# Each output tile stored as two transfers of 64 rows instead of one of 2 x 64 rows

## The chip, the cores and the metric

The kernel runs on one core of a Trainium2 chip. The metric is the time of one execution on the device in microseconds; the time of before is the median of three runs. One further execution was recorded by the hardware profiler, and all rows below are from it. TensorE (PE, with PEld for its weight loads), VectorE (DVE), ScalarE (ACT) and GpSimd (POOL) compute; SyncE (SP) issues nearly all DMAs, which 16 DMA engines carry out. "SPq" and "ACTq" in a row are the queues of SP and ACT, with their DMA issues; "q1" is the DMA queue that SP's issues go to, "q10" that of ACT's.

## The reference, cut to what matters

A gated linear recurrence over 768 steps for 4 batches and 8 heads of 40 elements, and then a feed-forward block with a rational activation on the 3072 tokens:

```python
for t in range(S):                       # for every batch and head
    m_new = np.maximum(f_gate[:, :, t] + m, i_gate[:, :, t])
    C = f_stab * C + i_stab * outer(v[t], k[t])
    n = f_stab * n + i_stab * k[t]
    y[:, :, t] = sigmoid(o_gate[t]) * (C @ q[t]) / np.maximum(np.abs(n @ q[t]), 1.0)
x = y.transpose(0, 2, 1, 3).reshape(B * S, H * D)      # [3072, 320]
h = x @ w_in                                           # [3072, 2048]
g = (a[0] + a[1]*h + a[2]*h**2 + a[3]*h**3) / (1 + abs(b[0])*abs(h) + abs(b[1])*h**2 + 1e-6)
out = g @ w_out                                        # [3072, 320], rows (batch, position)
```

## The kernel before, in words

The recurrence is computed in chunks of 64 positions, as matrix products with decay factors. The feed-forward block runs over twelve groups of 256 tokens (`SIZES`), each in eight steps over 256 of the 2048 hidden columns: a product into `ph` with `w_in`, some ten operations on ACT, DVE and POOL for the activation, and a product that adds into `po` with `w_out`. Weights and activations are kept as a high and a low part, so that each product is several matmuls. Loads, recurrence and feed-forward of different groups are interleaved by the text `ORDER`, a list of steps written out beforehand; every engine works through its own steps in that order, and SP too: a DMA that waits holds up the DMAs behind it. SP's DMAs use eight semaphores in turn, so that an issue also waits until the transfer eight places ahead has landed.

A group covers two batches and 128 positions. It ends with two output tiles `ot` (t = 0 and 1), each of 128 partitions and 320 columns: partitions 0 to 63 hold 64 positions of one batch, partitions 64 to 127 the same positions of the next. In `out` the rows of the two batches lie 768 rows apart. Step `ev` (`f_ev`) moves `po` from PSUM to the tile, on ACT for most groups; step `ed` (`f_ed`) issues its store from SP. For the very last tile of the last group `ev` is on DVE, and `f_ev` calls `f_ed` itself with ACT's queue. Line 34 of the profile is the helper that records every operation in order; the store from ACT has line 1353, in `f_ed`. At the end the program waits on SP for all stores (line 1469). A flag read from the input chooses between two versions of the program; the rows are of the version that ran.

Of the kernel before, what the change touches and what calls it, by code (L numbers as in the profile page):

```python
# [374 lines left out]
def _program(  # L375
# [16 lines left out]
    nc = _Ordered(tc)  # L392
    B, H, S, D = q.shape
    DM, DFF = w_in.shape
    P = 128
    L = 64
# [48 lines left out]
    def ring(pool, tag, shape, name, dt=F32, at=None):  # L445
        k = plan.slot[tag] if at is None else at
        return pool.tile(shape, dt, tag=f"{tag}{k}", name=name, bufs=1)
# [767 lines left out]
    def feed_forward(n, i):  # L1215
        d = {}
# [83 lines left out]
        def parts_of(t):  # L1300
            return [(t, 0, 0, DM)] if t < 8 - BANKS else [(0, DM, 0, 512 - DM), (1, DM, 512 - DM, DM)]
# [28 lines left out]
        def f_ev(t, engine):  # L1330
            ot = d["ot", t] = ring(fp, "ot", [P, DM], f"ot{n}_{t}")
            for b, at, lo, hi in parts_of(t):
                to, po = ot[:, lo:hi], PO[n, half][b][:, at : at + hi - lo]
                if split:
                    nc.vector.scalar_tensor_tensor(
                        to, po, pa[:, 3:4] if square else 1.0, PT[n][:, t, lo:hi], op0=ALU.mult, op1=ALU.add
                    )
                elif engine == "DVE":
                    nc.vector.tensor_scalar(to, po, pa[:, 3:4] if square else 1.0, None, op0=ALU.mult)
                elif square:  # L1340
                    nc.scalar.activation(to, po, AF.Copy, scale=pa[:, 3:4])
                else:
                    nc.scalar.copy(to, po)
            if engine == "DVE" and not split:
                f_ed(t, nc.scalar)

        def f_ed(t, queue):
            m = firsts_of[n] + t // 2
            blk, b = divmod(2 * m, B)
            rows = out.rearrange("(b s) e -> b s e", b=B)[  # L1350
                b : b + 2, blk * P + t % 2 * L : blk * P + (t % 2 + 1) * L
            ]
            queue.dma_start(rows, d["ot", t])

        k = f"{n}_{i}"
        a0, a1 = (ps[:, 2:3], ps[:, 1:2]) if square else (pa[:, 0:1], pa[:, 1:2])
# [1 line left out]
        def add(name, engine, cost, fn, r=(), w=(), new=(), part=None, **kw):  # L1358

            def own(x):  # L1360
                if x not in ("h", "ha", "w", "p", "gH", "gL"):
                    return x
                if part is None or not last:
                    return f"{x}{k}"
                return f"h{k}p{part}" if x == "h" else f"{x}{k}.{part}"

            plan.add(
                f"{name}{'half' if last and part is not None else ''}_{k}", engine, cost, fn,
                [own(x) for x in r], [*(own(x) for x in w), f"turn {name}"],
                [(own(x).split(".")[0], t) for x, t in new], **kw,  # L1370
            )
# [10 lines left out]
        for j in range(2):  # L1382
            f = chunk(j)
            add("f1", "PE", 0.9, lambda j=j: f_f1(j), w=["h"], new=[("h", ("h", BANKS))] if j == 0 or last else (), part=j,
                r=[*xs, f"wi{f // 2}", f"wi{f // 2}.l",
                   *(f"wj{f % 8 // 4}{x}" for x in ("", ".x", ".l"))])
# [24 lines left out]
        if i == NS - 1:  # L1411
            for t in range(groups):
                o = f"ot{n}_{t}"
                e = "DVE" if split or t == groups - 1 and n == len(SIZES) - 1 else "ACT"
                add("ev", e, 0.32, lambda t=t, e=e: f_ev(t, e), r=[f"pt{n}.{t}"] if split else [],
                    w=[*(po[b] for b, *_ in parts_of(t)), o], new=[(o, ("ot", BUFS["ot"]))], lag=2.5)
                if e == "ACT" or split:
                    add("ed", "SP", 0.6, lambda t=t: f_ed(t, nc.sync), r=[o], lag=2.5)

    stg = ctx.enter_context(tc.tile_pool(name="stage", bufs=2))  # L1420
    ap1 = ctx.enter_context(tc.tile_pool(name="att1", bufs=1))
# [17 lines left out]
    for n, i in steps + [(n, i) for n in range(SPLIT, len(SIZES)) for i in range(NS)]:  # L1439
        feed_forward(n, i)  # L1440
# [33 lines left out]
```

## Time and profile before

| what | value |
|---|---|
| runs | 507.96, 509.19, 509.38 us; median 509.19 us |
| profiled execution, span from first to last instruction | 504.4 us |
| TensorE busy | 478.4 us, 95% of the span |
| output stores | 24 of 160 KB: 23 issued from SP, 1 from ACT |
| first and last of SP's stores issued at | 126.4 us and 493.1 us |

The profiled execution is given by its span alone; its own time, with what lies before the first and after the last instruction, is not recorded. The runs lie 3.5 to 4.9 us above the span. A DMA issue has a start and a length on the queue of its engine; the transfer itself is seen only in the views of the DMA engines, which show their busy share and the bytes moved.

### The profile page before, as it was taken

What the parts mean: (1) busy time and instruction counts of PE and PEld (TensorE: products, weight loads), DVE (VectorE), ACT (ScalarE), POOL (GpSimd) and SP (SyncE); (2) the same over time, 40 slices, a digit from 0 to 9 for tenths busy, and PEclk for the clock granted to TensorE, in tenths of its full rate; (3) what the DMA queues carried; (4) which work ended last, traced back from release to release, by engine and by line L of the source; (5) the groups of instructions that cost most, each with busy time, mean ns of one, the idle gap of its engine ahead of it and who ended that gap; (6) DMA issues with size and microseconds to landing.
All of it is one profiled execution on the core that took longest, in us unless ns stands there. A gap on an engine that the chain in (4) does not pass through costs nothing.

```text
span 504.4 us, 14192 instructions
## 1 busy us (share of the span) xinstructions
PE 478.4 (95%) x5631; PEld 462.5 (92%) x5631; DVE 420.4 (83%) x716; ACT 402.1 (80%) x698; POOL 385.4 (76%) x365
## 2 busy tenths in 40 slices
PE   5988889999999999999999999999999999999990
PEld 5977778999999999999999999999999999999980
DVE  7787999999998898897868887796977998687890
ACT  3488999898986886879887799797788778779960
POOL 2767689998868878877888788878868887967760
PEclk9989999999999999999999999999999999999996
DMA  6899998503543335333326522320332030000001
GB/s 177 192 198 232 234 219 163 101 12 66 106 111 77 71 80 105 82 73 83 52 72 116 115 58 59 79 57 6 64 97 44 3 74 3 18 10 2 27 1 33
DMA packets 119438, 42.54 MB, mean 84 GB/s; under 512 B 103618, under 2 KB 111874, under 8 KB 119362
## 3 DMA queue, kind: packets, MB, share of 16 engines
q1 hardware_dynamic: 119232, 41.37, 38.0%
q8 instruction: 46, 0.75, 0.6%
q14 instruction: 30, 0.25, 0.1%
q10 hardware_dynamic: 130, 0.16, 0.1%
HBM read 36.90 MB, written 4.10 MB: 81 GB/s over the span
## 4 chain that ended last, share of the span: by engine, by line
PE 72%; DVE 8%; ACT 5%; DMA 4%; POOL 3%; issue 3%; SPq 3%; DVEq 0%; ACTq 0%; POOLq 0%
PE ph L34 30%; PE po L34 29%; PE y L34 4%; PE kq L34 3%; SPq L34 3%; PE ow L34 3%; PE ps L34 2%; DMA kr<-in_k_dram 2%; POOL p L34 1%; PE px L34 1%; DMA rawj<-in_moe_w_in_dram 1%; ACT ph L34 1%; DVE w L34 1%; DVE gH L34 1%; DMA rawi<-in_moe_w_in_dram 1%
## 5 line engine op out<-in xcount | busy, mean ns | idle before, releaser
L34 POOL TENSOR_TENSOR p<-p,w 128x512 f32<-128x512 f32 (+1 forms) x97 | 127.6, 1316 | 59.7 <-DVE w L34 55.8
L34 PE MATMUL ph<-xk,wi 128*128 128x256 f32 x1152 | 167.8, 281 | 0.5 <-DVE zo L34 0.5
L34 PEld LDWEIGHTS ph<-xk,wi 128*128 128x128 f32 x1152 | 149.8, 188 | 1.9 <-PE ph L34 0.7
L34 POOL TENSOR_TENSOR w<-w,ha 128x512 f32<-128x512 f32 (+1 forms) x97 | 127.1, 1316 | 10.0 <-ACT w L34 9.9
L34 PE MATMUL po<-wo,gH 128*128 128x320 f32 x768 | 134.6, 312 | 0.0
L34 PEld LDWEIGHTS po<-wo,gH 128*128 128x128 f32 x768 | 115.1, 188 | 0.8
L34 DVE SCALAR_TENSOR_TENSOR gL<-p,ps,ph 128x512 fp32r<-128x512 f32 (+1 forms) x97 | 71.3, 735 | 22.0 <-POOL p L34 19.8
L34 DVE SCALAR_TENSOR_TENSOR w<-w,gH 128x512 f32<-128x512 f32 (+1 forms) x97 | 81.7, 842 | 4.1
L34 ACT ACTIVATE ph<-w,cd 128x512 f32<-128x512 f32 (+1 forms) x97 | 66.6, 687 | 22.7 <-POOL w L34 12.4
L34 DVE SCALAR_TENSOR_TENSOR gH<-p,ps,ph 128x512 fp32r<-128x512 f32 (+1 forms) x97 | 71.3, 735 | 13.9 <-ACT ph L34 12.9
L34 ACT ACTIVATE w<-ha,ba 128x512 f32<-128x512 f32 (+1 forms) x97 | 78.6, 813 | 2.3
L34 ACT ACTIVATE ha<-ph 128x512 f32<-128x512 f32 (+1 forms) x97 | 57.5, 593 | 27.4 <-PE ph L34 26.6
L34 PE MATMUL po<-wo,gL 128*128 128x320 f32 x384 | 77.2, 314 | 0.8 <-DVE gL L34 0.8
L34 DVE SCALAR_TENSOR_TENSOR p<-p,ps,ph 128x512 f32<-128x512 f32 (+1 forms) x97 | 70.5, 734 | 7.2 <-ACT p L34 6.9
L34 ACT ACTIVATE p<-ph,ps 128x512 f32<-128x512 f32 (+1 forms) x97 | 65.2, 679 | 0.3
L34 PEld LDWEIGHTS po<-wo,gL 128*128 128x128 f32 x384 | 59.2, 188 | 2.3 <-DVE gL L34 1.7
L34 ACT ACTIVATE ph<-ph 128x512 f32<-128x512 f32 (+1 forms) x97 | 56.0, 578 | 2.2
L34 PE MATMUL ph<-xk,wY 128*128 128x256 f32 x192 | 53.5, 279 | 0.0
L34 PE MATMUL ph<-xk,wj 128*128 128x256 f32 x192 | 53.4, 278 | 0.0
L34 PEld LDWEIGHTS ph<-xk,wj 128*128 128x128 f32 x192 | 36.1, 188 | 0.0
L34 PEld LDWEIGHTS ph<-xk,wY 128*128 128x128 f32 x192 | 36.1, 188 | 0.0
L34 PE MATMUL hot<-ident 128*128 128x128 f32 x180 | 25.0, 297 | 4.0 <-DVE flag_out L370 4.0
(136 smaller groups left out, 650.2 us busy)
## 6 DMA issues: line engine op xcount, KB each, us to landing
rawo<-in_moe_w_out_dram SPq DMA_DIRECT2D x8, 640.0 KB
ab<-scrA SPq DMA_DIRECT2D x40, 128.0 KB
rawi<-in_moe_w_in_dram SPq DMA_DIRECT2D x8, 512.0 KB
kr<-in_k_dram SPq DMA_DIRECT2D x24, 160.0 KB
vb<-in_v_dram SPq DMA_DIRECT2D x48, 80.0 KB
og<-in_o_gate_dram SPq DMA_DIRECT2D x48, 80.0 KB
qn<-in_q_dram SPq DMA_DIRECT2D x24, 160.0 KB
out_dram<-ot SPq DMA_DIRECT2D x23, 160.0 KB
```

Source lines behind the costliest of these rows:

```text
L34: made = fn(*args, **kwargs)
```

## The change

`f_ed` takes a list of queues, one for each batch, and issues one store of 64 rows for each: rows 0 to 63 of the tile to one batch, rows 64 to 127 to the next. From SP both go out one behind the other; for the last tile the first half goes out from ACT and the second from SP.

```diff
             if engine == "DVE" and not split:
-                f_ed(t, nc.scalar)
-
-        def f_ed(t, queue):
+                f_ed(t, (nc.scalar, nc.sync))
+
+        def f_ed(t, queues):
             m = firsts_of[n] + t // 2
             blk, b = divmod(2 * m, B)
-            rows = out.rearrange("(b s) e -> b s e", b=B)[
-                b : b + 2, blk * P + t % 2 * L : blk * P + (t % 2 + 1) * L
-            ]
-            queue.dma_start(rows, d["ot", t])
+            at = blk * P + t % 2 * L
+            for j, queue in enumerate(queues):
+                rows = out.rearrange("(b s) e -> b s e", b=B)[b + j, at : at + L]
+                queue.dma_start(rows, d["ot", t][j * L : (j + 1) * L])
...
-                    add("ed", "SP", 0.6, lambda t=t: f_ed(t, nc.sync), r=[o], lag=2.5)
+                    add("ed", "SP", 0.6, lambda t=t: f_ed(t, (nc.sync, nc.sync)), r=[o], lag=2.5)
```

SP's issues at the end of the program, from the loads of the last chunks of the recurrence (`kr`, `qn`, `vb`, `ab`) to the last DMA of this version; `ot_0` and `ot_1` are the two output tiles of a group, and the numbers behind them only tell tiles apart. Before:

```order
L34 DMA out_dram<-ot_1_5859 2x64x320
L34 DMA vb_62<-in_v_dram 64x8x40 x2
L34 DMA ab_6447<-scrA 64x2x256 x2
L34 DMA out_dram<-ot_0_6382 2x64x320
L34 DMA out_dram<-ot_1_6384 2x64x320
L34 DMA vb_129<-in_v_dram 64x8x40 x2
L34 DMA out_dram<-ot_0_6914 2x64x320
L34 DMA out_dram<-ot_1_6916 2x64x320
L34 DMA out_dram<-ot_0_7360 2x64x320
L34 DMA out_dram<-ot_1_7383 2x64x320
L34 DMA out_dram<-ot_0_7657 2x64x320
```

The same piece of SP's queue with the change:

```order
L34 DMA out_dram<-ot_1_5873 64x320 x2
L34 DMA vb_62<-in_v_dram 64x8x40 x2
L34 DMA ab_6463<-scrA 64x2x256 x2
L34 DMA out_dram<-ot_0_6398 64x320 x2
L34 DMA out_dram<-ot_1_6400 64x320 x2
L34 DMA vb_129<-in_v_dram 64x8x40 x2
L34 DMA out_dram<-ot_0_6932 64x320 x2
L34 DMA out_dram<-ot_1_6934 64x320 x2
L34 DMA out_dram<-ot_0_7380 64x320 x2
L34 DMA out_dram<-ot_1_7403 64x320 x2
L34 DMA out_dram<-ot_0_7679 64x320 x2
L34 DMA out_dram<-ot_1_7683 64x320
```

Every store of SP has become two, at the same place in the queue, and one more of the last tile stands at the end.

ACT's last rows, from the last activations of the last group to its branch. Before:

```order
L34 ACTIVATE ph_7_1_7582<-w_7_7573,cd 128x256
L34 ACTIVATE ph_7_1_7582<-ph_7_1_7582 128x256
L34 ACTIVATE ot_0_7657<-po_0_0_7402,pa 128x320
L1353 DMA out_dram<-ot_1_7660 2x64x320
L319 UNCONDITIONAL_BRANCH
```

And with the change:

```order
L34 ACTIVATE ph_7_1_7602<-w_7_7593,cd 128x256
L34 ACTIVATE ph_7_1_7602<-ph_7_1_7602 128x256
L34 ACTIVATE ot_0_7679<-po_0_0_7422,pa 128x320
L1353 DMA out_dram<-ot_1_7683 64x320
L319 UNCONDITIONAL_BRANCH
```

The store on ACT stays where it was and has half of the tile. On the other engines no row is moved, added or removed.

## Rows read from the trace of the kernel before

**Rows 1.** The page: span; busy us, share of it and instructions per engine.

```profile
span 504.4 us, 14192 instructions
...
PE 478.4 (95%) x5631; PEld 462.5 (92%) x5631; DVE 420.4 (83%) x716; ACT 402.1 (80%) x698; POOL 385.4 (76%) x365
```

**Rows 2.** Busy time by stretches: length, engines with instructions, granted clock, DMA share, GB/s.

```profile
126.00:493.00 367.00, 365.79 (x4129) 356.46 (x4127) 308.59 (x481) 301.34 (x516) 292.99 (x267) 1.00 0.28 60
493.00:504.40 11.40, 0.00 (x0) 0.00 (x0) 0.28 (x1) 0.10 (x1) 0.00 (x0) 0.60 0.12 37
```

**Rows 3.** Timeline from 492.5 us: start, length, operation, [idle before <-releaser].

```profile
492.12 0.56 PE L34 MATMUL po<-wo,gL 128*128 128x320 f32 x2
492.58 0.53 ACT L34 ACTIVATE ot<-po,pa 128x320 f32<-128x320 f32 x1 [2.89 <-PE po L34]
492.73 0.55 DVE L34 TENSOR_SCALAR ot<-po,pa 128x320 f32<-128x320 f32 x1 [0.66 <-PE po L34]
493.13 0.51 SPq L34 DMA_DIRECT2D out_dram<-ot  x1
493.31 1.29 ACTq L1353 DMA_DIRECT2D out_dram<-ot  x1
```

**Rows 4.** SP's waits from 440 us: total us, times, longest us.

```profile
SPq L1469 <- DMA out_dram<-ot: 9.4, 2, 7.0
```

**Rows 5.** DMA, 493 to 505 us: slices of 0.3 us; queues: packets, MB.

```profile
DMA  0030111111013211101111111111110000000000
GB/s 0 0 82 27 26 36 51 26 26 34 21 30 93 79 51 70 43 30 47 53 43 51 47 47 51 51 47 51 47 51 34 21 27 0 0 0 0 0 0 0
...
q1 hardware_dynamic: 130, 0.16, 4.8%
q10 hardware_dynamic: 130, 0.16, 3.9%
q14 instruction: 7, 0.06, 1.4%
```

**Rows 6.** DMA, 436 to 444 us, two stores of SP; slices of 0.2 us.

```profile
DMA  0201101011010114111111111111111111111102
GB/s 26 26 13 51 38 19 32 32 38 32 26 26 32 51 51 127 51 51 51 51 45 45 51 51 51 51 45 51 45 51 51 51 51 51 45 51 45 51 13 82
...
q1 hardware_dynamic: 260, 0.33, 12.5%
```

**Rows 7.** DMA queues from 493 to 497.6 us.

```profile
q1 hardware_dynamic: 88, 0.11, 9.4%
q14 instruction: 5, 0.04, 2.7%
```

**Rows 8.** Timeline of SP's issues from 285 us.

```profile
285.75 1.11 SPq L34 DMA_DIRECT2D g<-scrF  x2
```

**Rows 9.** DMA from 285.5 to 290 us: 40 slices of 0.1125 us.

```profile
DMA  9999431221210044444444653441000005000000
GB/s 225 223 189 150 68 36 10 18 13 9 23 18 11 16 164 164 164 182 164 164 164 182 237 182 146 164 146 55 36 18 0 0 0 146 0 0 0 0 0 0
```

**Rows 10.** Timeline of SP's issues from 402 us.

```profile
402.08 1.33 SPq L34 DMA_DIRECT2D vb<-in_v_dram  x2
403.51 1.76 SPq L34 DMA_DIRECT2D ab<-scrA  x2
405.36 1.21 SPq L34 DMA_DIRECT2D out_dram<-ot  x2
406.67 3.63 SPq L34 DMA_DIRECT2D vb<-in_v_dram  x2
```

**Rows 11.** Compute engines' waits for a DMA, 126 to 493 us.

```profile
POOL p L34 <- DMA og<-in_o_gate_dram: 0.9, 1, 0.9
```

**Rows 12.** The tensor out_dram: issues, ns min/median/max, first and last start.

```profile
L34 SPq DMA_DIRECT2D out_dram<-ot x23: 511/571/810, 126.4 to 493.1; - x23
```

## Prediction

> **What bounds the kernel now.** I read the page first: a span of 504.4 us with TensorE busy for 95% of it [rows 1]. So the next question is where TensorE is not busy, and the table by stretches answers it [rows 2]: from 126 us, when the first output tile is stored, to 493 us it is busy for 365.79 of 367.00 us at a granted clock of 1.00, and from 493 to 504.4 us it does nothing at all. The end of the program is therefore 11.4 us in which no engine computes. The timeline shows what it is made of [rows 3]: ACT and DVE evict the last two tiles until 493.1 and 493.3, SP issues the store of one at 493.13, ACT that of the other at 493.31, and no row comes after these two. SP's own waits name what it stands in: the end of the program waits twice for out_dram<-ot, 9.4 us together, the longer 7.0 [rows 4]. From the end of SP's issue (493.13 + 0.51 = 493.64) this makes 503.0 us for the last landing; the remaining 1.4 us to 504.4 close the program.
>
> Why do two stores of 160 KB take that long? The DMA view of the tail [rows 5] has slices of 0.3 us. The stores move from about 494.2 us to 502.6 us at some 50 GB/s (the last slice with bytes, 27 GB/s for 0.3 us, is 8 KB: a fetch of instructions, not a store). The share of 16 engines is one or two tenths, and each queue shows 130 packets for a tile of 128 rows. Two stores back to back in the middle of the run, with nothing else moving but two fetches of instructions, show it cleaner [rows 6]: 260 packets of q1 take 12.5% of 16 engines in 8 us, which is 2.0 engines, and the rate settles at 51 GB/s, 25 GB/s an engine. So a store of both batches runs on two engines, however idle the other fourteen are, and the two last stores share the same two: the pair of streams together moves no faster than 51 GB/s.
>
> **The change, part by part.** A store now has 64 rows on both sides as its first dimension, where it had 2 (batches) on the side of HBM and 128 partitions on the other. No store of that form is in the trace; the nearest rows are loads, g<-scrF, also 64 rows each. SP issues two of them at 285.75 in 1.11 us [rows 8], and their rows move between about 287.1 and 288.9 us mostly at 146 to 182 GB/s and a share of four tenths, six at most, that is 6 to 10 engines [rows 9]. So 64-row transfers do not stay on two engines, and 262 KB went in 1.8 us, 0.9 us for each transfer of 131 KB.
>
> In the Trainium skill, DMA: Bandwidth & Descriptors, in the section on why a DMA increments its semaphore by 16 and not by 1, gives a rule for this: a DMA issued from SP or ACT runs on the largest number of engines up to 16 that divides the slowest dimension of both sides, 2 before and 16 after. By that rule the data of one half would take an eighth of the time per byte that it takes now. The trace agrees on the 2 (130 packets are 128 rows and 2 more; 2.0 engines); the 16 for a store no row here shows.
>
> The new tail, in steps:
> 1. Issues. SP had one at 493.13 and now has three (two halves of the first tile, one of the second), ACT keeps one. A pair of stores on SP takes 1.21 us [rows 10], 0.6 each, and the median of all 23 is 0.571 [rows 12]. Three end at 493.13 + 1.8 = 494.9 if ACT's does not disturb them. ACT's took 1.29 beside one of SP's [rows 3]; if all four follow one another, the last ends at 493.13 + 1.8 + 1.29 = 496.2. I take 495.4, nearer the first, since the two issues now overlap almost completely.
> 2. From the end of the last issue to its last row. For the loads of rows 8 and 9 the first row moved 1.3 us after the first issue began, so some 0.7 us after an issue of 0.6 ends; 82 KB at their rate are 0.56 us. That gives 1.25 as the lower bound. The upper one is what the pair showed from the end of its second issue, 288.9 - 286.9 = 2.0. I take 1.5. The last row leaves at 496.9.
> 3. Landing and closing, as before: 502.6 to 504.4, 1.8 us. The span ends at 498.7. With the wait for the rows nearly gone, it is the issues that set the end.
>
> That is 5.7 us less than 504.4. The bounds are 494.9 + 1.25 + 1.8 = 498.0 (6.4 less) and 496.2 + 2.0 + 1.8 = 500.0 (4.4 less). One more thing could hold ACT's half: up to 497.6 us no packet of q10 is in the trace, although ACT's issue ended at 494.6; only q1 moved [rows 7]. Either ACT's store stood behind SP's, whose 128 rows were still being worked off (then this goes too), or ACT's queue needs 3 us on its own (then its half starts at 497.6, ends 0.5 later, and the span ends at 499.9, inside the upper bound). The first is likelier, because SP shows it too: two loads vb issued behind two stores took 3.63 us where a pair takes 1.33 [rows 10].
>
> Before the tail, SP gets 22 more issues of 0.6 us, 13 us spread over 367, and the loads in its queue behind a store are issued 0.6 us later, 1.2 behind a pair. What they had in front of them was worse: two of the engines were occupied for 3 to 4 us per store with its rows. The price of either is bounded by who waits for loads: from 126 to 493 us the only compute engine that does is POOL, once, 0.9 us for og [rows 11], and TensorE has 1.2 us of idle time in all [rows 2]. I set it to nothing: TensorE's queue of work covers it. If this cover were gone, the issues of 0.6 us would come onto the path one by one; if og's wait goes, at most 0.9 us are won. The eight semaphores of SP's DMAs are used up faster by two stores per tile, but each is free again when its transfer has landed, which is now earlier.
>
> **The profiled execution** is given only by its span, 504.4; the runs are 507.96, 509.19 and 509.38, so 3.5 to 4.9 us lie around it. I take this as unchanged and subtract from the median: 509.19 - 5.7 = 503.5 us, with bounds 502.8 and 504.8.
>
> **The rivals.**
> *No spreading where it counts.* The two halves cost an issue each and move no faster, because stores into HBM are held to about 50 GB/s by something other than the count of engines. For it: stores that move alone settle at 51 GB/s and no higher [rows 6]. Against it: they all have the form of before, and 2.0 engines at 25 GB/s explain the rate alone. Time: the stores end when they did, plus at most 1.2 us of issues, 509.2 to 510.4; most of it inside what a measurement can tell from no change. In the Trainium skill, DMA: Bandwidth & Descriptors, section Rules for kernel authors, says not to split a transfer into halves by partitions, since both run on all 16 engines anyway and queue behind each other. By that rule this rival would hold; but the trace disagrees with its ground, since the one transfer runs on 2.0 engines.
>
> *One engine in place of two (slower).* A half is 64 x 1280 bytes without a gap in HBM; if the transfer is handled as one run, all of it goes to a single engine. Then the last two tiles, 328 KB at 25 GB/s, move from 494.2 to 507.3, and the span ends at 509.1, 4.7 later: 513.9 us. It decides as soon as a half uses fewer than two engines. For it only the gapless address; against it the 64 separate rows on the other side and the loads of rows 9.
>
> *Loads late.* The extra issues push the loads behind stores past their need, in the bursts where SP issues ten transfers without pause. Half of the 22 reaching TensorE with 0.3 us each would give back 3.3 us: 506.8. For it: SP's queue is in order. Against it: rows 11.
>
> **How the numbers follow.** Forecast 0.87 (503.5, own range 502.0 to 505.5); no spreading 0.05; one engine 0.03; loads late 0.05, which is still faster than before. About 0.3%, 1.5 us, is what a measurement of this kernel can tell from no change. Faster 0.92, same 0.05, slower 0.03. The range 501.8 to 505.6 takes the bounds of the sum, 502.8 to 504.8, og's 0.9 us below, and the scatter of the runs.
>
> **What would show it.** In the profile after: q10 with 80 packets (64 and 16) in place of 130; a tail from 493 to about 498.7 with rates above 100 GB/s between 494.5 and 497; SP's waits for out_dram at the end near 2 us in place of 9.4; everything before 493 us within 1 us of where it was. Wrong would be: a tail of 50 GB/s (no spreading), of 25 (one engine), or a last eviction after 494.5 us (loads late).

## The result, and the profile after

The kernel with the change takes 500.98 us, the median of 4 runs (500.23 to 501.46), beside 508.83 us for 4 runs of the kernel before (507.96 to 509.38): a ratio of 0.9852 [0.9809, 0.9895]. (The ratios come with 95% intervals and need not be the quotient of the two medians, which is 0.9846 here.) Two later comparisons of the same two kernels gave 0.9890 [0.9858, 0.9922] and 0.9885 [0.9846, 0.9924]. So the change makes the kernel faster by a little over 1%; by the later two ratios that is 5.6 and 5.8 us. The forecast was 503.5 us with a range from 501.8: the side was right, the time lies 0.8 us below the range.

The page of the kernel after, and its busy time by stretches (columns as in [rows 2]):

```profile
span 498.4 us, 14219 instructions
```

```profile
126.00:493.00 367.00, 364.99 (x4121) 355.64 (x4119) 308.10 (x480) 300.82 (x515) 292.41 (x266) 1.00 0.30 60
493.00:498.40 5.40, 0.00 (x0) 0.00 (x0) 0.00 (x0) 0.00 (x0) 0.00 (x0) 0.86 0.32 74
```

From 126 to 493 us TensorE is busy for 364.99 us where it was 365.79 (in this trace the last eviction begins 0.74 us sooner, so that the stretch's end already belongs to the tail). The last stretch is 5.4 us long where it was 11.4, and its DMA share is 0.32 where it was 0.12.

The timeline from 491.5 us, answering to [rows 3]:

```profile
491.84 0.53 ACT L34 ACTIVATE ot<-po,pa 128x320 f32<-128x320 f32 x1 [2.89 <-PE po L34]
491.99 0.55 DVE L34 TENSOR_SCALAR ot<-po,pa 128x320 f32<-128x320 f32 x1 [0.66 <-PE po L34]
492.39 1.95 SPq L34 DMA_DIRECT2D out_dram<-ot  x3
492.57 0.56 ACTq L1353 DMA_DIRECT2D out_dram<-ot  x1
```

SP issues three halves in 1.95 us, ACT one in 0.56 (its whole store took 1.29 before). The DMA view from 493 us to the end, in slices of 0.135 us, answering to [rows 5]:

```profile
DMA  2004789997999138773410000002000000200000
GB/s 61 0 0 108 171 171 171 218 218 152 232 218 199 48 76 209 152 161 108 121 61 0 0 0 0 0 0 61 0 0 0 0 0 0 61 0 0 0 0 0
...
q1 hardware_dynamic: 240, 0.25, 21.0%
q10 hardware_dynamic: 80, 0.08, 6.7%
q14 instruction: 7, 0.06, 3.4%
```

The share rises to nine tenths and the rate to 232 GB/s. The stores move from 493.4 to 495.7 us (slices 3 to 19; the 61 GB/s of the next are 8 KB, a fetch of instructions), where it took them 8 us. Each half has 80 packets, 64 rows and 16 more, where a tile had 128 rows and 2 more. By the rule of the Trainium skill (DMA: Bandwidth & Descriptors, the section on why a DMA increments its semaphore by 16 and not by 1) a half would run on 16 engines; the 16 additional packets and the share of nine tenths agree.

SP's waits at the end, answering to [rows 4], are no longer for a DMA; the only ones of the closing line are these:

```profile
SPq L1469 <- PEq L1469: 0.6, 2, 0.5
```

What ends last now? The stores' last rows move at 495.7, yet the span ends at 498.4. Nor is it their landing: the DMA view from 493.75 us, which holds SP's last issue alone, gives 2.2 us from that issue (493.8) to its landing, and 2.7 from ACT's (492.6), so all has landed by 496.0:

```profile
out_dram<-ot SPq DMA_DIRECT2D x1, 80.0 KB, 2.2
```

The instructions of two source lines on SP tell what it is: line 319 is the jump at the end of the program's first version, over the code of the second; line 1469 is the closing. Columns: count, ns min/median/max, first and last start. The first fence is the kernel after, the second the kernel before.

```profile
L1469 SPq EVENT_SEMAPHORE  x10: 17/28/28, 497.1 to 498.4; - x10
...
L319 SPq COMPARE_BRANCH  x2: 38/44/49, 4.1 to 494.4; - x2
```

```profile
L1469 SPq EVENT_SEMAPHORE  x10: 17/28/28, 500.7 to 504.4; - x10
...
L319 SPq COMPARE_BRANCH  x2: 43/46/49, 4.1 to 493.7; - x2
```

After: SP jumps at 494.4 and its first closing instruction is at 497.1, 2.7 us later, with no wait for a DMA in between and 1.1 us after the last landing; what still moves once the rows are gone is the instruction queues (the single slices of 61 GB/s, 8 KB each). So the reading is that SP waits for its code behind the jump, and the kernels with a short jump below test it. Before, it was 7.0 us from jump to first closing instruction, and that was the wait for the first of the two stores; a fetch of some 3 us fits under it, as the kernel with halves in all but the last group shows below. The tensor out_dram, answering to [rows 12]:

```profile
L34 SPq DMA_DIRECT2D out_dram<-ot x47: 467/588/1633, 125.5 to 493.8; - x47
L1353 ACTq DMA_DIRECT2D out_dram<-ot x1: 556/556/556, 492.6 to 492.6; - x1
```

47 issues in place of 23, the median one about as long as before (0.588 against 0.571 us). And the wait of POOL that could have moved [rows 11] is 0.8 us, on another load:

```profile
POOL p L34 <- DMA ab<-scrA: 0.8, 1, 0.8
```

### The profile page after: what moved, and what is told of

The parts are those of the page before. It is cut to its first block, busy times and chain, and to the rows that moved or that the text cites. A ratio compares the mean times of both kernels' runs of the same rounds, so it can differ in the third digit from the quotient of the medians.

```text
span 498.4 us, 14219 instructions
## 1 busy us (share of the span) xinstructions
PE 478.1 (96%) x5631; PEld 462.1 (93%) x5631; DVE 421.9 (85%) x716; ACT 402.5 (81%) x698; POOL 385.8 (77%) x365
## 4 chain that ended last, share of the span: by engine, by line
PE 73%; DVE 7%; ACT 5%; DMA 4%; issue 3%; POOL 3%; SPq 3%; DVEq 0%; ACTq 0%; POOLq 0%
PE ph L34 30%; PE po L34 29%; PE y L34 4%; PE kq L34 3%; PE ow L34 3%; SPq L34 2%; PE ps L34 2%; DMA kr<-in_k_dram 2%; POOL p L34 2%; PE px L34 1%; DMA rawo<-in_moe_w_out_dram 1%; ACT ph L34 1%; DMA rawi<-in_moe_w_in_dram 1%; DVE w L34 1%; DVE gH L34 1%
```

## The experiments

Theory: a store whose first dimension in HBM is the two batches runs on two engines, one of 64 rows on sixteen; only the last two tiles matter, because nothing waits for the others. Rivals: the gain comes from the middle (the two engines are free sooner for loads); or it comes from two transfers being in flight in place of one, whatever their form. Three kernels change or leave out part of the work: the one with halves over both batches puts rows at other places of the output, and the two with a short jump lack the second version of the program, so that they compute the reference only where the flag chooses the first.

One table for all traces. "First store" and "last eviction" are starts; the tail runs from the end of the last eviction to the end of the span; the ratio is to the kernel before, run beside it.

| kernel | first store | last eviction | span | tail | ratio |
|---|---|---|---|---|---|
| before | 126.4 | 492.73 | 504.4 | 11.1 | |
| before again | 126.2 | 492.66 | 504.5 | 11.3 | 1.0008 [0.9993, 1.0023] |
| change | 125.5 | 491.99 | 498.4 | 5.9 | 0.9852 [0.9809, 0.9895] |
| change, second time | 126.4 | 492.85 | 499.4 | 6.0 | 0.9890 [0.9858, 0.9922] |
| change, third time | 127.6 | 494.03 | 501.4 | 6.8 | 0.9885 [0.9846, 0.9924] |
| halves in the last group only | 126.9 | 493.37 | 500.3 | 6.4 | 0.9905 [0.9878, 0.9932] |
| halves in all but the last group | 127.5 | 493.97 | 505.5 | 11.0 | 0.9997 [0.9983, 1.0011] |
| halves over both batches | 127.9 | 494.37 | 505.9 | 11.0 | 1.0001 [0.9984, 1.0019] |
| one wide store, reads reordered | 126.5 | 494.27 | 500.0 | 5.2 | 0.9924 [0.9898, 0.9949] |
| one wide store, writes reordered | 128.7 | 495.10 | 500.8 | 5.2 | 0.9887 [0.9849, 0.9926] |
| the same again | 126.4 | 492.87 | 498.6 | 5.2 | 0.9877 [0.9850, 0.9903] |
| two halves each on SP and ACT | 128.5 | 494.96 | 502.4 | 6.9 | 0.9877 [0.9853, 0.9901] |
| change, short jump | 129.4 | 495.90 | 501.4 | 5.0 | 0.9890 [0.9854, 0.9925] |
| wide store, short jump | 130.2 | 496.61 | 500.9 | 3.7 | 0.9846 [0.9819, 0.9873] |

From the first store to the last eviction it is 366.3 to 366.5 us in every row but one (367.8 with reordered reads). The first store itself lies anywhere from 125.5 to 130.2; what one execution's span has over another's of the same kernel was spent ahead of it, but for the differences in the tail (5.9 to 6.8 us for the change).

**The kernel before again**, unchanged, as a control.

> The kernel before, unchanged, timed against itself, to see span and time of each run. If what lies around the span is a constant, time minus span is 1.8 us as in the changed kernel's four runs (500.23 - 498.4, 501.46 - 499.7), and the profiled span of 504.4 was of an execution some 2 us faster than the median; then spans here are near 506 to 507. If the change also shortened what lies outside the span, time minus span is 3.5 to 4.5 us here. Ratio 1.000 within 0.3%.

Its profiled run took 506.53 us with a span of 504.5: 2.0 us lie around the span. Its 12 runs reach from 506.53 to 510.12, and the 23 runs of the kernel before beside them from 506.26 to 509.81, median 507.47. The 507.96 to 509.38 us on which the prediction stood were three runs from the upper half of this.

**The change, second and third time.**

> The whole change once more, in the same call as the other three, for its interval: 0.985 to 0.989 if the tail of 5.3 us less is all of it (5.3 of 508.8 is 0.9896), below 0.987 if something beyond the tail was won too.

> The change a third time, for the size of the gain: the traces give 5.2 to 5.3 us between the first of the last issues and the end of the span, a ratio of 0.9895; the first comparison gave 0.9852 and the second 0.9890. If the first one caught the runs before at the high end of their scatter (506.3 to 509.8 us) and the change's at the low end of its own, this gives 0.988 to 0.991; if there is a second gain of some 2 us outside the tail, 0.984 to 0.987.

They take 501.87 and 503.13 us (6 runs each, together 499.45 to 504.98). The gain stands; its size scatters with the first store and, by 0.9 us, with the tail. The timeline of the third shows where half of the latter comes from: SP's three issues took 2.43 us there instead of 1.95. The rest lies behind its jump, 3.1 us to the first closing instruction (496.9 to 500.0) instead of 2.7:

```profile
494.44 2.43 SPq L34 DMA_DIRECT2D out_dram<-ot  x3
494.61 0.55 ACTq L1353 DMA_DIRECT2D out_dram<-ot  x1
```

**Halves in the last group only, and in all but the last.** In `f_ed`, ahead of the loop (`<` in the first, `==` in the second):

```diff
+            if n < len(SIZES) - 1:
+                rows = out.rearrange("(b s) e -> b s e", b=B)[b : b + 2, at : at + L]
+                queues[0].dma_start(rows, d["ot", t])
+                return
```

> Only the last group's two tiles are stored in halves, the other 22 tiles as before. Theory (all of the gain is in the tail, because the last rows move on more than two engines): the same gain as the whole change, ratio 0.985 to 0.989, last eviction to end of span 5.9 us as in the changed kernel (11.2 before). Rival (part of the gain, up to 2 us, comes from loads in the middle that no longer queue behind stores): ratio 0.989 to 0.993.

> The opposite: 22 tiles in halves, the last two as before. Theory: no gain, ratio 0.998 to 1.002, tail of 11.2 us; 22 more issues on SP's queue cost nothing that reaches TensorE. Rival (loads in the middle gain): ratio 0.995 to 0.998, the last eviction 1 to 2 us earlier.

The first has the gain, 0.9905, its interval overlapping that of the change run beside it; the second has none, 0.9997 [0.9983, 1.0011]. The stretches of the second:

```profile
127.00:494.00 367.00, 366.04 (x4130) 356.65 (x4128) 308.46 (x482) 301.36 (x516) 293.34 (x267) 1.00 0.29 60
494.00:505.50 11.50, 0.00 (x0) 0.00 (x0) 0.52 (x1) 0.35 (x1) 0.00 (x0) 0.64 0.12 36
```

Its middle is as long as any, with 22 tiles stored by halves, and its tail is that of the kernel before. So the 22 earlier tiles neither give nor cost anything that can be measured, and the rival of the middle falls.

This trace also shows the fetch apart from the wait. SP jumps at 495.1 and its first closing instruction (line 1473 here) stands at 497.9, 2.8 us later, when the stores are far from done; its two waits for them come behind it:

```profile
SPq L1473 <- DMA out_dram<-ot: 6.3, 2, 4.5
```

**Halves over both batches.** Two transfers per tile, but each with the two batches as its first dimension:

```diff
-                rows = out.rearrange("(b s) e -> b s e", b=B)[b + j, at : at + L]
+                rows = out.rearrange("(b s) e -> b s e", b=B)[b : b + 2, at + 32 * j : at + 32 * (j + 1)]
```

> Two transfers of 64 rows per tile as in the change, but each takes 32 rows of both batches, so that its first dimension on the side of HBM is 2 again; the rows land in other places of the output than the reference's. Theory (the form of a transfer sets how many engines carry it, and that alone makes the gain): each queue shows 64 rows and 2 packets more per transfer, the stores move at some 50 GB/s, and the tail is back at 11.2 us or up to 1.2 us longer; ratio 1.000 to 1.003. Rival (two transfers instead of one make the gain, whatever their form): ratio 0.989, tail of 5.9 us.

The ratio is 1.0001: the number of transfers is that of the change, and nothing is gained. Its DMA view from 495 us, slices of 0.275 us, and SP's wait at the end:

```profile
DMA  0011111112031211120111111111111110000000
GB/s 0 0 60 19 9 9 33 47 33 58 23 111 51 67 51 51 42 83 5 42 42 47 56 47 47 51 51 47 47 56 47 47 51 34 0 0 0 0 0 0
...
q1 hardware_dynamic: 198, 0.25, 7.2%
q10 hardware_dynamic: 66, 0.08, 2.3%
```

```profile
SPq L1469 <- DMA out_dram<-ot: 8.1, 2, 6.3
```

66 packets are 64 rows and 2 more, the share is one tenth, the rate 51 GB/s, as in [rows 5]. It is the first dimension on the side of HBM, not the number of transfers.

**One wide store.** If form is all, one transfer of a whole tile with 64 as its first dimension must do as well. Its rows alternate between the two batches, so they do not lie one behind the other in HBM as those of a half do; if it is as fast, a gapless address is not the cause either. The positions of both batches are interleaved within a tile (partition 2s + b), and the order is made where tokens are transposed into `px`, first by reading the identity in another order, in steps of 64 columns (`px` 1 is changed in the same way):

```diff
+            mixed = ident.rearrange("p (j s) -> p s j", j=2)
...
-                    transpose(d["px", 0][:, i * T + c * P : i * T + (c + 1) * P], xf[:, i * P : (i + 1) * P])
+                    nc.tensor.transpose(d["px", 0][:, i * T + c * P : i * T + (c + 1) * P], xf[:, i * P : (i + 1) * P], mixed)
...
-            for j, queue in enumerate(queues):
-                rows = out.rearrange("(b s) e -> b s e", b=B)[b + j, at : at + L]
-                queue.dma_start(rows, d["ot", t][j * L : (j + 1) * L])
+            rows = out.rearrange("(b s) e -> s b e", b=B)[at : at + L, b : b + 2]
+            queues[0].dma_start(rows, d["ot", t])
```

> One transfer per tile as before, but with 64 as first dimension on the side of HBM: the tokens of a tile are interleaved (position, batch) by a reordered identity in the transposes that make xk, so that row 2s+b of the tile belongs to position s of batch b. Theory (form, not number): the tail is as short as the change's or shorter, 5.0 to 5.9 us, ratio 0.985 to 0.990, with SP's and ACT's issues at one each, 130 packets becoming 144 per tile. If a transfer of 128 rows were itself the cause of the slow tail, the tail stays at 11.2 us. The reordered identity costs nothing if the transposes take as long as before.

The tail is 5.2 us, but the middle is 1.3 us longer, and the ratio 0.9924. The tile px names the cost: the 72 transposes take 301 ns with the identity read so, 273 in the kernel with the change, which reads it in order. The second version therefore reorders at the place that the transposes write, every second column (`px` 1 likewise, and the store as above):

```diff
-                    transpose(d["px", 0][:, i * T + c * P : i * T + (c + 1) * P], xf[:, i * P : (i + 1) * P])
+                    transpose(d["px", 0][:, i * T + c * P : i * T + (c + 1) * P].rearrange("p (s j) -> p j s", j=2), xf[:, i * P : (i + 1) * P])
...
```

> One wide transfer per tile as in the kernel wide_exact, but the reordering is in the addresses to which the transposes write, not in the identity that they read, which made 72 transposes 301 ns in place of 273. If that was why wide_exact needed 367.8 us from the first store to the last eviction in place of 366.5, this is back at 366.5 and the ratio is 0.987 to 0.990, 0.7 us faster than the change in the tail (5.2 against 5.9 us). If the writes are as slow, 0.992 again.

> The wide transfer with reordered addresses a second time, for its interval against the change's 0.985 to 0.989: from the traces 0.7 to 1.6 us faster than the change, ratio 0.985 to 0.9885; the difference from the change is below what the intervals can tell.

The tile px with reordered reads, and then with reordered writes:

```profile
L34 PE MATMUL px<-ident,xn x72: 296/301/351, 48.1 to 452.0; 128*128 128x128 f32 x48, 128*64 128x128 f32 x24
```

```profile
L34 PE MATMUL px<-ident,xn x72: 272/272/331, 49.6 to 452.8; 128*128 128x128 f32 x48, 128*64 128x128 f32 x24
```

The DMA view of the version with reordered writes from 495 us, slices of 0.145 us:

```profile
DMA  0004000200218999994410000401000000101000
GB/s 0 0 0 113 0 0 0 56 0 0 56 53 282 335 353 283 344 309 159 175 44 26 9 0 0 113 0 56 0 0 0 0 0 0 56 0 56 0 0 0
...
q1 hardware_dynamic: 144, 0.16, 9.1%
q10 hardware_dynamic: 144, 0.16, 8.5%
```

144 packets are 128 rows and 16 more, and both tiles leave at up to 353 GB/s with one issue from SP and one from ACT. The middle is back at 366.4 us. 0.9887 and 0.9877 are the change's ratio within the intervals; in the traces the tail is 0.7 to 1.6 us shorter. So a gapless address is not needed. SP has no wait for a store at its end here either, and its first closing instruction stands 3.4 us behind its jump (496.1 to 499.5), so the fetch still ends last. The Trainium skill says, in DMA: Bandwidth & Descriptors, section Rules for kernel authors, that one transfer is to be preferred to two halves. The tails agree for the one transfer with 64 as its first dimension (5.2 us against 5.9 to 6.8), while the ratios cannot tell the two apart; for the one of before, which ran on two engines, the rule does not hold (11.1 us).

**Two halves each on SP and ACT.** If SP's three issues set the end, two on either queue should end sooner:

```diff
-                    add("ed", "SP", 0.6, lambda t=t: f_ed(t, (nc.sync, nc.sync)), r=[o], lag=2.5)
+                    add("ed", "SP", 0.6, lambda t=t: f_ed(t, (nc.sync, nc.scalar if n == len(SIZES) - 1 else nc.sync)), r=[o], lag=2.5)
```

> The change, with the second half of the last but one tile issued from ACT instead of SP, so that SP and ACT have two issues each at the end. Theory (the new end is set by SP's last issue and what SP does after it, not by the last landing): SP's last issue ends 0.6 us earlier and the tail shortens from 5.9 to 5.2 to 5.4 us. Rival (the last landing sets the end): the tail stays within 0.2 us of 5.9.

Neither figure came: the tail is 6.9 us. The timeline, ACT's two issues (ns min/median/max) and the two lines of SP:

```profile
495.37 1.85 SPq L34 DMA_DIRECT2D out_dram<-ot  x2
495.37 2.02 ACTq L1353 DMA_DIRECT2D out_dram<-ot  x2
```

```profile
L1353 ACTq DMA_DIRECT2D out_dram<-ot x2: 555/990/1425, 495.4 to 496.0; - x2
```

```profile
L1469 SPq EVENT_SEMAPHORE  x10: 17/28/28, 500.8 to 502.3; - x10
...
L319 SPq COMPARE_BRANCH  x2: 38/44/49, 4.1 to 497.3; - x2
```

Four issues take 2.02 us from the first to the last, as with three and one (1.95), and nothing is won. ACT's first issue took 0.56 us although SP's began with it, its second 1.43; what made the second long these runs do not show. SP's last issue thus ended hardly sooner than in the change (1.85 us after its first in place of 1.95), and the way from its jump to its first closing instruction took 3.5 us (497.3 to 500.8) in place of 2.7. So the premise that SP would be done sooner fell; that SP's last issue and what follows it set the end stands. The ratio, 0.9877, is not to be told from the change's.

**Short jump.** To see whether the fetch behind SP's jump is what ends last, the second version of the program is left out, so that the jump leads a short way:

```diff
         with tc.If(flag > 0) as test:
             _program(tc, True, common, *args)
-        with test.Else():
-            _program(tc, False, common, *args)
```

> The change without the second version of the program (the one for inputs whose flag is 0, which does not run here; the kernel is right only for inputs like these). At its end every engine jumps over that version to the closing code. Theory (after the last landing the end waits until SP has its closing instructions, 2.7 us after its jump in the change's traces): with nothing to jump over, SP is ready when the last rows have landed, and the time from the last row to the end of the span falls from 2.9 us to the 1.8 to 1.9 us of before; the tail falls from 5.9 to some 4.9 us. Rival (the 2.9 us are the landing of rows from sixteen engines): the tail stays at 5.9.

The two lines of SP, its waits, and the packets of the instruction queue from 496 us, for this kernel (its closing line is 1467):

```profile
L1467 SPq EVENT_SEMAPHORE  x10: 17/28/28, 499.0 to 501.3; - x10
...
L319 SPq COMPARE_BRANCH  x2: 43/46/49, 4.1 to 498.1; - x2
```

```profile
SPq L1467 <- DMA out_dram<-ot: 1.4, 2, 0.8
SPq L1467 <- PEq L1467: 0.6, 2, 0.5
```

```profile
q14 instruction: 1, 0.01, 0.6%
```

From jump to first closing instruction it is 0.9 us in place of 2.7, and up to 0.8 of this is itself a wait for a store: SP waits for the stores again, 1.4 us together. One instruction packet moves in the tail where there were seven. The tail is 5.0 us instead of 5.9 to 6.8. So in the kernel with the change the fetch is the last thing, and the landing lies under it. In the median it does not show (0.9890): the saving is less than the scatter of the first store, which was at 129.4 in this trace.

**Wide store and short jump together**, the two shortenings of the tail at once.

> Both improvements on the change together: one wide transfer per tile with reordered transposes, and no second version of the program to jump over (right only for inputs like these). If issues, rows and the wait for closing code are three pieces in series, the time from the start of the last eviction to the end of the span is 4.3 to 4.9 us (5.5 with the short jump alone, 5.7 with the wide transfer alone, 11.7 before), ratio 0.984 to 0.988. If the two save the same piece, it stays at 5.5.

The lowest median of all, 499.43 us, 0.9846 [0.9819, 0.9873], though the interval overlaps that of the wide store alone; the profiled run was the longest of its six, 502.69 us, with the latest first store of the table. Its last issues and its DMA view from 496 us, slices of 0.125 us:

```profile
497.01 0.54 SPq L34 DMA_DIRECT2D out_dram<-ot  x1
497.19 0.66 ACTq L1350 DMA_DIRECT2D out_dram<-ot  x1
```

```profile
DMA  0000000000000000029999999300000000000000
GB/s 0 0 0 0 0 0 0 0 0 0 0 0 0 0 0 0 0 72 307 410 358 338 338 358 338 103 0 0 0 0 0 0 0 0 0 0 0 0 0 0
```

The rows start at 498.1, 0.3 us after ACT's issue ends, and are gone by 499.3; 1.6 us of landing and closing follow. That is the tail of 3.7 us, or 4.3 us from the start of the last eviction, as expected of pieces in series. It is a version for one kind of input only; the wide store alone is what could be used in general.

## Why the prediction was right, and where it failed

**What bounds the kernel, and why the store is slow**: right. All the gain that these runs can tell comes from the last group, and it comes from the first dimension of the transfer, which four forms tell apart (130 and 66 packets at 51 GB/s, 80 and 144 at up to 232 and 353).

**The step that failed is the base**: "3.5 to 4.9 us lie around it. I take this as unchanged and subtract from the median: 509.19 - 5.7 = 503.5 us". Where a run has both its time and its span, 1.8 us lie around it for the change and 2.0 for the kernel before. So the profiled execution of before, with 504.4, took about 506.4 us and was a shorter one than the three runs shown; what was taken for time around the span was the difference between executions, and the median of three stood for a kernel that scatters over 5 us. All 78 runs of the kernel before, over all comparisons, reach from 505.05 to 510.12, with a median of 507.7, and all 16 of the change have a median of 501.6. Of the 2.5 us by which the forecast lay too high, 1.5 are thus the base (509.19 against 507.7), 0.4 the gain (6.1 against 5.7), and 0.6 that the 4 runs with 500.98 were low in their turn (beside them the medians lie 7.9 us apart, more than either repeat gives). The range had the same fault: it took the scatter from three runs that lay 1.4 us apart. The gain itself was forecast well: 503.5 is 0.9888 of 509.19, which lies inside all three measured intervals. That 506.4 - 5.7 = 500.7 comes close to 500.98 is luck, one short execution set against four short ones.

**The sum for the tail** came out close, by errors that partly cancel. Its parts, in the first trace of the change:

- Step 1, from the first issue to the end of the last: 2.27 us predicted, 492.39 + 1.95 = 494.34, so 1.95 measured (1.75 to 2.43 over the traces of this form). It was right here not to let ACT's issue follow at full length.
- Step 2, to the last row: 1.5 predicted, 495.7 - 494.34 = 1.4 measured.
- Step 3, "landing and closing, as before": 1.8 predicted, 498.4 - 495.7 = 2.7 measured. This is the term of the sum that was mis-sized. With the wait for the stores gone, the 2.7 us from SP's jump to its first closing instruction (494.4 to 497.1) are on the path. The short jump shows it. "It is the issues that set the end" was right in so far as SP's jump stands behind its last issue.

Together the tail from first issue to end is 6.0 us where 5.57 was predicted and 11.27 stood before, so the tail gives 5.3 us of the 5.7. The span fell by 6.0, since the last eviction also began 0.74 us sooner, along with a first store 0.9 us sooner, which the second and third run of the change do not show again. Over all traces of either tail (four of 11.0 to 11.3, three of 5.9 to 6.8) the gain is 4.9 us; the intervals of the second and third ratio contain that, that of the first (5.3 to 9.7 us) does not. Whether the gain in time is 4.9 or 6 us, these runs leave open.

**ACT's half**: "needs 3 us on its own" falls. ACT's issue ended at 493.13 and all rows, those of q10 among them, were gone by 495.7; 3 us of its own would have let them begin at 496.1. That it "stood behind SP's store" is what remains of the two and fits; no run tests it by itself.

**The middle, set to nothing**: right, 0.9997 [0.9983, 1.0011] with 22 tiles by halves.

**The rivals.** *No spreading*: 232 GB/s against the 50 it would need. *One engine*: the same rate. *Loads late*: the middle is 366.5 us long in the kernel after and 366.3 before; nothing of the 3.3 us. What had been named as signs came (80 packets in q10, rates above 100 GB/s, the middle within 1 us), but SP's waits for the stores did not fall to 2 us, they vanished, and that pointed to the fetch.

## What to carry to other kernels

Count the packets of a transfer and read its share of the engines: in these traces rows and 2 more, at a tenth of the share, meant that two engines carried it, and the outermost dimension on the side of HBM was the one to change, by halves or by a layout that lets one transfer have many rows outermost. Here it paid where nothing else ran, at the end of the program, and not under a busy TensorE. Before subtracting a gain from a median, find out how long the profiled execution itself took and how far executions scatter, and after removing a wait look for what had been hidden under it.

## What the runs showed of the hardware that was not expected

- SP reached the code behind the jump over the program's second version 2.6 to 3.5 us after it where no wait for a store covered it (496.3 to 498.9 with halves in the last group only, 494.4 to 497.1 with the change, 497.3 to 500.8 with two halves on either queue). With the second version left out it was 0.9 us, most of it a wait for a store.
- A DMA issue that takes 0.5 to 0.6 us alone can take two to three times as long at the end of the program: ACT's store took 1.29 us in the kernel before, and with two halves on either queue ACT's second took 1.43. It is not enough that the other engine issues at the same time, since ACT's first took 0.56 beside SP's; the cause stays open.
- A transpose whose identity is read in steps of 64 columns takes 301 ns; one whose output is written to every second column takes 272, as one in order does (273 in the kernel after).
